# A chunked recurrence feeding two gated matmul stages: masks in one slot, the output product two tiles behind, less work ahead of step 0, and step 1's diagonals from a second set of scores

## The chip, the core and the metric

The kernel runs on one core of a Trainium2 chip. The metric is device time in microseconds (us), the median of three runs: 926.12 us before the change (925.85 to 927.89). The engines are named as in the profile: PE (TensorE), DVE (VectorE), ACT (ScalarE), POOL (GpSimd) and SP (SyncE, which issues the DMAs). Each works through its own instructions in order, and waits where an instruction's input or buffer is not ready.

## What is computed

```python
# attention-like recurrence: B=4, H=8, S=768, D=48
for t in range(S):
    cur = outer(u * k[t], v[t])                 # per head, 48x48
    y[t] = r[t] @ (state + cur)
    state = w[:, None] * state + outer(k[t], v[t])
x = y as (3072 tokens, 384)
x = (x @ w_a * x @ w_b) @ w_out                 # 384 -> 1536 -> 384
out = ((x @ w1 * x @ w2) @ w3) @ w_out2         # 384 -> 1024 -> 1024 -> 384
```

The matmul weights arrive as 64-bit floats.

## The kernel before

The recurrence is cut into 6 chunks of 128 time steps. A **unit** u = 4c + b is chunk c of batch b. For a unit the kernel computes all heads' 128x128 scores on PE (`scores`), multiplies them on DVE with a triangular mask (`a_evac`, two halves of four heads), puts the diagonal, which carries `u` in place of the decay, into them on DVE (`a_diag`, two predicated copies), and then on PE adds the state's share and the scores' share to y (`y_mm`) and forms the state's update (`s_mm`). ACT and DVE move y out of PSUM (`y_evac`), ACT decays the state (`s_decay`), DVE adds the update (`s_upd`). The diagonal's values come from `prep_d`: two POOL products and one DVE reduce. `prep_r` and `prep_k` scale r and k by powers of w, `k_nat` does it for the state's update. All of a unit's PSUM results share two buffers named `at`, so each new result waits until DVE or ACT has emptied the one two places earlier. For chunk 0 a **first block** ahead of everything does the same without a state, and takes the diagonals from a second set of scores, made with u*k (`scores_d`, `diag_0`).

**Phase 1** has six **steps** q of 512 tokens. A step is 12 tiles f of the hidden width. For each there are two *ab tiles* of nine 128x512 matmuls on PE (w_a and w_b, each in high and low float32r parts); ACT copies the first out (`g`), DVE multiplies (`ab<-g,ab`), ACT rounds to the high part (`gh`), DVE subtracts for the low part (`gl`). An *m tile*, nine more matmuls with w_out, uses gh and gl, one tile behind. During step q the units of chunk q+1 run as side work.

**The weights** are turned from 64-bit floats into pairs of float32r on the fly, in jobs of 128x512: 27 for phase 1. A job is a load; on DVE L96, L112 and L115 (bits to float32), on ACT the rounded high part (L128) and two checks (L131, L150), on DVE the low part (L148). `step()` finishes the oldest job (L148) and begins the next (L112, the L96 of the job after, L115); `cast()` issues the ACT part. An ab tile needs its three `wab` jobs; the jobs stand in the order wab0 (3), wout0 (3), wab1 (3), wab2 (3), and so on.

**The order of the work** is written out by hand. `merge` walks a step's main slots (12 x 2 ab slots and the m slots), spreads the side slots evenly over them, and in step 0 also the remaining jobs, as pairs of `step` and `cast`. A unit has eight side slots (`unit_slots`). So what an engine does between two dependent instructions is what this weaving put there.

In the first block one job begins per unit. After it come three more steps (`TAIL`), `s_mm` and `s_upd` of units 0 and 1, and three of four preparation slots of unit 4; then step 0 starts, with `s_mm` of units 2 and 3 woven in first. POOL has no other work than the preparations, and runs them as soon as their inputs are there, wherever they stand in the program.

Of the kernel before, what the change touches and what calls it, by code (L numbers as in the profile page):

```python
# [7 lines left out]
F32 = mybir.dt.float32  # L8
# [29 lines left out]

WARM, WARM_0 = 10, 6


STEPS_U = (1, 0, 0, 0)
STEPS_K = (0, 1, 1, 1)
TAIL = (1, 2)

S_NOW = 2
PRE = 3

END_0 = 4
LATE = 3  # L50
# [5 lines left out]
class Stream:  # L56
# [97 lines left out]
    def step(self):  # L154
        self.finish()
        self.begin()
# [9 lines left out]
def rwkv_moe_kernel(ctx, tc, rkT, nat, wu, wab, wout, w12, w3T, wo2, r_in, k_in, v_in, w_in, u_in, out):  # L166
# [7 lines left out]
    def flat(ap):  # L174
        return ap.rearrange("p a b -> p (a b)")

    with tc.manual_schedule():
# [41 lines left out]
        wt, ut = wt[:, 0], wt[:, 1]  # L219
        load_rk(0)  # L220
        load_nat(0)
        u_bc = const.tile([128, DM], F32, name="u_bc")

        chk = const.tile([128, N64, 2], F32, name="chk")
        small = const.tile([128, 1], F32, name="small")
# [16 lines left out]
            for k in range(KD):  # L242
                wab_ready[i] = st.add(wab[i, :, k, :], lambda k=k: dst(k))

        def add_wout(i):
# [5 lines left out]
            for j in range(3):  # L251
                s = slice(j * 512, (j + 1) * 512)
                wo_ready[i] = st.add(flat(wout[i])[:, s], lambda s=s: dst(s))

        def add_w12(i):
            w12_t[i] = [w12p.tile([128, KD, 512], F32R, name=f"w12{p}{i}") for p in "hl"]
            for k in range(KD):
                w12_ready[i] = st.add(w12[i, :, k, :], lambda k=k: [t[:, k, :] for t in w12_t[i]])

        for i in range(6):  # L260
            add_wab(i)
            if i % 2 == 0:
                add_wout(i // 2)
        st.AHEAD = 1
        for u in range(1, B):
            load_rk(u)
# [5 lines left out]
        def later_loads(u):  # L272
# [7 lines left out]
            elif u == 3:  # L280
# [8 lines left out]
        mask = const.tile([128, 128], F32, name="mask")  # L289
# [30 lines left out]
        tr = const.tile([112, NP, C], F32, name="tr")  # L320
        nc.vector.tensor_copy(out=tr[:, :, HALF:], in_=pos[:, :, 0:HALF])
        nc.vector.reciprocal(out=tr[:, :, 0:HALF], in_=pos[:, :, 1:][:, :, ::-1])
        tk = const.tile([112, NP, C], F32, name="tk")
        nc.vector.tensor_copy(out=tk, in_=tr[:, :, ::-1])
        wC = const.tile([112, NP, 1], F32, name="wC")
        nc.vector.tensor_tensor(out=wC, in0=pos[:, :, HALF:], in1=pos[:, :, HALF:], op=ALU.mult)
        s_t = [att.tile([112, NP, 112], F32, name=f"s{b}", bufs=1) for b in range(B)]

        rf_t, d_t, a_t, kn_t, at_ps, xt = {}, {}, {}, {}, {}, {}

        kf_t, pr_t, y3_t = {}, {}, {}

        def prep_r(u, eng):
            r = rk_t[u][:, 0, :]
# [116 lines left out]
        def s_mm(u):  # L451
            c, b = divmod(u, B)
            v = v_of(u)
            nat_t.pop(u, None)
            if c == NC - 1:
                return
            ps = (ps_at.tile([112, NP, D], F32, name="at") if c else
                  ps_m.tile([112, NP, D], F32, tag=("m2", "m0")[u % 2], name="s_ps"))
            at_ps["s", u] = ps
# [25 lines left out]
        def prep_slots(u):  # L485
            return [
                lambda: (prep_r(u, nc.gpsimd), prep_k(u, nc.vector)),
                lambda: prep_d(u, 0),
                lambda: prep_d(u, 1),
                lambda: prep_d(u, 2),  # L490
            ]

        def unit_slots(u):
            n = u + 1
            nxt = n < NU
            pool = nc.gpsimd

            def after(f, *a):
                if nxt:
                    f(n, *a)  # L500

            return [
                lambda: (scores(u), after(prep_r, pool)),
                lambda: (a_evac(u, 0), after(prep_k, pool)),
                lambda: (a_evac(u, 1), a_diag(u, 0), k_nat(u)),
                lambda: a_diag(u, 1),

                lambda: (y_mm(u), s_mm(u)),
                lambda: (load_rk(u + 2), load_nat(u + 2), y_evac(u), (u + 1) % B == 0 and y_shuffle(u // B), s_decay(u),
                         after(prep_d, 0)),  # L510
                lambda: (s_upd(u), after(prep_d, 1)),
                lambda: after(prep_d, 2),
            ]

# [46 lines left out]
            a_evac(u, 0)  # L561
            a_evac(u, 1)

        def steps(n):
            for _ in range(n):
                step()
                st.cast()

        prep_0(0)
        warm_up(WARM_0)  # L570
        scores_0(0)
# [8 lines left out]
        for u in range(B):  # L580
            if u + 1 < B:
                scores_0(u + 1)
                scores_d(u + 1)
            y_0(u)
            if u + 2 < B:
                prep_0(u + 2)
            if u + 1 < B:
                both_a(u + 1)
                diag_0(u + 1)
            y_0_evac(u)  # L590
            steps(STEPS_U[u])
            later_loads(u)
            if u == 2:
                tn_ps = ps_m.tile([128, NP, 112], F32, tag="m0", name="tn_ps")
                for p in range(NP):
                    mm(tn_ps[:, p, :], lhsT=tkw[:, p, :], rhs=ident[:112, :112], start=True, stop=True)
                tnat = const.tile([128, NP, 2, D], F32, name="tnat")
# [12 lines left out]


        def ab_mm(ps, w, cs, x):
# [6 lines left out]
        def ab_slots(x, wget, keep):  # L619

            t = {}

            def run_a():
                w, ca, _ = wget()
                t["a"] = ps_ab.tile([128, TB], F32, name="ab")
                ab_mm(t["a"], w, ca, x())

            def run_b():
                w, _, cb = wget()
                t["b"] = ps_ab.tile([128, TB], F32, name="ab")  # L630
                ab_mm(t["b"], w, cb, x())

            def evac_a():
                t["g"] = gp.tile([128, TB], F32, tag="g", name="g")
                nc.scalar.copy(out=t["g"], in_=t["a"])  # L635

            def evac_b():
                g = t["g"]
                gh = gp.tile([128, TB], F32R, tag="gh", name="gh")
                gl = gp.tile([128, TB], F32R, tag="gl", name="gl")  # L640
# [29 lines left out]

        def m_evac(q):
            for k in range(KD):
                t = gp.tile([128, TB], F32, tag=("g", "gh", "gl")[k], name="m_sb")
                nc.scalar.copy(out=t, in_=m_ps[q][k])
                nc.sync.dma_start(out=m_d[q][:, k, :], in_=t)

# [46 lines left out]
        for q in range(NB):  # L723
            main = []
            for f in range(NF1):
                main += ab_slots(lambda q=q: xt[q], lambda q=q, f=f: w1_get(q, f),
                                 lambda *t, q=q, f=f: gt.__setitem__((q, f), t))
                lag.append((q, f))
                if len(lag) > 1:
                    main.append(m_slot(*lag.pop(0)))  # L730
            side = step_slots(q + 1)
            if q == 0:
                side = [lambda u=u: (s_mm(u), s_upd(u)) for u in range(S_NOW, B)] + prep_slots(B)[PRE:] + side
            if q == 0:
                late = [step, st.cast] * (len(st.jobs) - st.begun + 1)
                late += [lambda: None] * (len(late) // LATE)
# [359 lines left out]
```

## Time and profile before

| | us |
|---|---|
| median of three runs | 926.12 |
| the profiled execution | 927.42 |
| its span, first to last instruction | 925.7 |
| PE busy in the span | 888.2 (96%) |
| DVE busy | 447.2 (48%) |
| ACT busy | 327.7 (35%) |
| POOL busy | 122.0 (13%) |

The shares are means over stages that differ. The first 33 us are the first block; step 0 runs until 156 us; after that PE is never without work until the last results leave, at some 919 us. A row of the timeline gives start, duration, engine, line, operation, result and inputs; in square brackets the engine's idle time ahead of it and what ended that. Consecutive like instructions are merged with a count, and instructions overlap a little at their ends, so the pace is read from start to start. PEclk is the granted TensorE clock as a share of 2.4 GHz.

### The profile page before, as it was taken

The numbers are of one execution on the slowest core, as the hardware profiler recorded it, in microseconds if no ns is written. First come the engines' busy times: TensorE is split into PE (matmuls) and PEld (weight loads), VectorE is DVE, ScalarE is ACT, GpSimd is POOL, SyncE is SP. The second block draws the span as 40 slices with busy tenths as digits, with TensorE's granted clock in tenths as the row PEclk, the third lists the DMA queues.
The fourth block names the chain that finished last, engine by engine and source line by source line (L and its number), as shares of the span: only waits on it lengthen the run. The fifth ranks groups of instructions, "written<-read, shape, count | busy, mean of one in ns | idle before, by whom it ended". The sixth has DMA issues, their size and how long they took to land.

```text
span 925.7 us, 12522 instructions
## 1 busy us (share of the span) xinstructions
PE 888.2 (96%) x4962; PEld 753.1 (81%) x4962; DVE 447.2 (48%) x745; ACT 327.7 (35%) x737; POOL 122.0 (13%) x118
## 2 busy tenths in 40 slices
PE   8488879999999999999999999999999999999997
PEld 7366668888888888888888888899988888888886
DVE  8889894444334433443333789676332323222212
ACT  4375563322222223222121687655322212122211
POOL 2512322222222312320300000000000000000000
PEclk9789989999999999999999999999999999999999
DMA  8545432211222212222103345442020201010001
GB/s 250 180 142 170 145 114 63 80 46 59 65 66 64 78 47 71 66 64 64 62 2 106 127 146 189 143 146 95 12 69 0 69 1 57 12 35 1 35 0 38
DMA packets 26066, 73.57 MB, mean 79 GB/s; under 512 B 3152, under 2 KB 7376, under 8 KB 26000
## 3 DMA queue, kind: packets, MB, share of 16 engines
q1 hardware_dynamic: 26000, 72.70, 25.2%
q8 instruction: 41, 0.67, 0.3%
q14 instruction: 25, 0.20, 0.1%
HBM read 61.28 MB, written 9.44 MB: 76 GB/s over the span
## 4 chain that ended last, share of the span: by engine, by line
PE 86%; DVE 8%; ACT 2%; DMA 2%; issue 2%; SPq 0%; ACTq 0%
PE ab L616 50%; PE m L667 5%; PE m L668 5%; PE m L669 5%; PE at L764 4%; PE o L788 3%; PE o L789 3%; PE o L787 3%; PE at L403 2%; PE at L363 2%; DVE cvt L112 2%; DVE cvt L115 2%; PE at L399 2%; DVE cvt L96 1%; DMA rk<-in_rkT_dram 1%
## 5 line engine op out<-in xcount | busy, mean ns | idle before, releaser
L641 DVE TENSOR_TENSOR ab<-g,ab 128x512 f32<-128x512 f32 x120 | 83.4, 695 | 301.2 <-PE ab L616 299.8
L616 PE MATMUL ab<-xt,w12h 128*128 128x512 f32 x576 | 177.4, 389 | 0.0
L635 ACT COPY g<-ab 128x512 f32<-128x512 f32 x120 | 70.0, 583 | 250.5 <-PE ab L616 250.5
L642 ACT CAST gh<-ab 128x512 fp32r<-128x512 f32 x120 | 70.3, 586 | 239.4 <-DVE ab L641 239.4
L616 PEld LDWEIGHTS ab<-xt,w12h 128*128 128x128 f32 x576 | 107.5, 188 | 18.8
L647 DVE TENSOR_TENSOR gl<-ab,gh 128x512 fp32r<-128x512 f32 x120 | 82.8, 690 | 65.7 <-ACT gh L642 65.5
L616 PE MATMUL ab<-xt,w12l 128*128 128x512 f32 x288 | 112.0, 389 | 0.0
L668 PE MATMUL m<-gl,woh 128*128 128x512 f32 x216 | 84.9, 393 | 1.5 <-DVE gl L647 1.5
L667 PE MATMUL m<-gh,woh 128*128 128x512 f32 x216 | 86.2, 399 | 0.0
L669 PE MATMUL m<-gh,wol 128*128 128x512 f32 x216 | 84.5, 391 | 0.0
L336 POOL TENSOR_TENSOR rk<-rk,tr 112x512 f32<-112x512 f32 x20 | 27.4, 1368 | 293.1 <-DMA rk<-in_rkT_dram 249.0
L616 PEld LDWEIGHTS ab<-xt,w12l 128*128 128x128 f32 x288 | 54.1, 188 | 11.3
L616 PE MATMUL ab<-xt,wab0h 128*128 128x512 f32 x144 | 48.5, 420 | 4.2 <-ACT xt L427 4.2
L668 PEld LDWEIGHTS m<-gl,woh 128*128 128x128 f32 x216 | 40.8, 189 | 11.1 <-DVE gl L647 2.7
L667 PEld LDWEIGHTS m<-gh,woh 128*128 128x128 f32 x216 | 40.8, 189 | 9.9 <-issue 0.4
L669 PEld LDWEIGHTS m<-gh,wol 128*128 128x128 f32 x216 | 40.7, 188 | 8.6
L115 DVE SCALAR_TENSOR_TENSOR cvt<-stg_t,cvt 128x512 int32<-128x512 int32 x61 | 47.0, 770 | 0.3
L112 DVE SCALAR_TENSOR_TENSOR cvt<-stg_t,cvt 128x512 int32<-128x512 int32 x61 | 46.9, 770 | 0.3
L616 PE MATMUL ab<-xt,wab1h 128*128 128x512 f32 x144 | 46.6, 405 | 0.0
L616 PE MATMUL ab<-xt,wab2h 128*128 128x512 f32 x144 | 45.9, 400 | 0.0
L616 PE MATMUL ab<-xt,wab3h 128*128 128x512 f32 x144 | 45.4, 396 | 0.0
L616 PE MATMUL ab<-xt,wab4h 128*128 128x512 f32 x144 | 45.3, 396 | 0.0
(271 smaller groups left out, 1579.6 us busy)
## 6 DMA issues: line engine op xcount, KB each, us to landing
natt<-in_nat_dram SPq DMA_DIRECT2D x20, 576.0 KB, 5.0
rk<-in_rkT_dram SPq DMA_DIRECT2D x24, 448.0 KB, 3.8
stg_t<-in_wab_dram SPq DMA_DIRECT2D x18, 512.0 KB, 3.7
stg_t<-in_w3T_dram SPq DMA_DIRECT2D x16, 512.0 KB, 3.6
stg_t<-in_w_dram SPq DMA_DIRECT2D x12, 512.0 KB, 3.7
stg_t<-in_wout_dram SPq DMA_DIRECT2D x9, 512.0 KB, 3.8
m_d<-m_sb SPq DMA_DIRECT2D x18, 256.0 KB, 2.2
stg_t<-m_d SPq DMA_DIRECT2D x18, 256.0 KB, 2.6
```

What stands on the lines that cost most here:

```text
L112: nc.vector.scalar_tensor_tensor(out=f, in0=w[:, :, 1], scalar=-0x40000000, in1=f, op0=ALU.bitwise_and, op1=ALU.bitwise_or)
L115: nc.vector.scalar_tensor_tensor(out=f, in0=w[:, :, 0], scalar=29, in1=f, op0=ALU.logical_shift_right, op1=ALU.bitwise_or)
L616: mm(ps, lhsT=w[i][:, k, cs], rhs=x[:, j, k, :], start=(n == 0), stop=(n == 3 * KD - 1))
L635: nc.scalar.copy(out=t["g"], in_=t["a"])
L641: nc.vector.tensor_tensor(out=t["b"], in0=g, in1=t["b"], op=ALU.mult)
L642: nc.scalar.copy(out=gh, in_=t["b"])
L647: nc.vector.tensor_tensor(out=gl, in0=t["b"], in1=gh, op=ALU.subtract)
L667: mm(m_ps[q][k], lhsT=wh[:, j, cs], rhs=gh, start=(f == 0), stop=False)
L668: mm(m_ps[q][k], lhsT=wh[:, j, cs], rhs=gl, start=False, stop=False)
L669: mm(m_ps[q][k], lhsT=wl[:, j, cs], rhs=gh, start=False, stop=(f == NF1 - 1))
L764: mm(f_ps[i], lhsT=w3_t[i][a][:, g, :], rhs=wo2_t[g // 4][b][:, g % 4, :], start=(n == 0), stop=(n == 3 * NF2 - 1))
L787: mm(o_ps[q][b], lhsT=ph[:, cs], rhs=wh, start=(f == 0), stop=False)
```

## The change

It has six parts. Line numbers in the diff's changed kernel are some 4 to 8 away from those before.

1. **First block.** `cast` goes ahead of `step`, one of each per unit; the three steps after it, its `k_nat`, `s_mm` and `s_upd` and the preparation of unit 4 are no longer there. They become side slots at the beginning of step 0, which has 42 side slots in place of 35 and 24 jobs left in place of 21.
2. **Jobs' order.** The first third of wout0 stands ahead of wab1, the other two behind it, and so on; an m tile of step 0 asks for the thirds it uses.
3. **Masks.** Both halves of the mask stand in one side slot.
4. **Diagonals of step 1** (units 4 to 7): as in the first block, from a second set of scores on PE (`scores_u`) with k scaled by u*w on ACT (`prep_u`); `prep_d`, with its two POOL products and its reduce, goes for these units. The predicated copies read PSUM.
5. **m two tiles behind** in every step, with three buffers for gh and gl.
6. Some constants move to a pool that is released after step 4.

```diff
-STEPS_U = (1, 0, 0, 0)
-STEPS_K = (0, 1, 1, 1)
-TAIL = (1, 2)
-S_NOW = 2
-PRE = 3
+STEPS = (1, 1, 1, 1)
...
         for i in range(6):
             add_wab(i)
-            if i % 2 == 0:
-                add_wout(i // 2)
+            add_wout(i // 2, ((0,), (1, 2))[i % 2])
...
+        def prep_u(u):
+            ku_t[u] = att.tile([112, NP * C], F32, name="ku", bufs=1)
+            for p in range(NP):
+                s = slice(p * C, (p + 1) * C)
+                nc.scalar.activation(out=ku_t[u][:, s], in_=kf_t[u][:, s], func=ACTF.Copy, scale=uw[:, p:p + 1])
+
+        def scores_u(u):
+            for x in range(2):
+                at_ps["d", u, x] = ps_at.tile([128, NP, C], F32, name="at")
+            scores_f([at_ps["d", u, x] for x in range(2)], flat(rf_t[u]), ku_t.pop(u))
...
+            if u < 2 * B:
+                return [
+                    lambda: (scores(u), after(prep_r, pool)),
+                    lambda: (a_evac(u, 0), a_evac(u, 1), after(prep_k, pool)),
+                    lambda: k_nat(u),
+                    lambda: scores_u(u),
+                    lambda: (diag_0(u), n < 2 * B and prep_u(n), n == 2 * B and prep_d(n, 0)),
+                    lambda: (y_mm(u), s_mm(u)),
+                    lambda: (load_rk(u + 2), load_nat(u + 2), y_evac(u), (u + 1) % B == 0 and y_shuffle(u // B),
+                             s_decay(u), n == 2 * B and prep_d(n, 1)),
+                    lambda: (s_upd(u), n == 2 * B and prep_d(n, 2)),
+                ]
...
-            steps(STEPS_U[u])
+
+            st.cast()
+            for _ in range(STEPS[u]):
+                step()
             later_loads(u)
...
-            for b in ((), (), (0, 1), (2, 3))[u]:
-                k_nat(b)
-            steps(STEPS_K[u])
-        steps(TAIL[0])
-        for u in range(S_NOW):
-            s_mm(u)
-            s_upd(u)
-        steps(TAIL[1])
-        for f in prep_slots(B)[:PRE]:
-            f()
...
-            if q == 0 and j == 0:
-                st.split(wo_ready[i])
+            if q == 0:
+                st.split(wo_ready[i, min(j, 2)])
...
-                if len(lag) > 1:
+                if len(lag) > 2:
                     main.append(m_slot(*lag.pop(0)))
             side = step_slots(q + 1)
             if q == 0:
-                side = [lambda u=u: (s_mm(u), s_upd(u)) for u in range(S_NOW, B)] + prep_slots(B)[PRE:] + side
+                side = ([lambda u=u: k_nat(u) for u in range(B)] + [lambda u=u: (s_mm(u), s_upd(u)) for u in range(B)] +
+                        prep_slots(B) + side)
```

What follows are stretches of the engines' order, before and after. On PE, ahead of and in the first ab tiles of step 0 (`s_ps`, later `at<-v,k`, is `s_mm`), before:

```order
L616 MATMUL ab<-xt,wab0h 128x512 x2
L616 MATMUL ab<-xt,wab0l 128x512
L464 MATMUL s_ps<-v_97,k_96 48x48 x8
L616 MATMUL ab<-xt,wab0h 128x512 x2
L616 MATMUL ab<-xt,wab0l 128x512
```

and now, after four ab tiles without anything between them:

```order
L620 MATMUL ab<-xt,wab0h 128x512 x2
L620 MATMUL ab<-xt,wab0l 128x512
L470 MATMUL at<-v_97,k_96 48x48 x8
L620 MATMUL ab<-xt,wab1h 128x512 x2
L620 MATMUL ab<-xt,wab1l 128x512
```

`s_mm` of unit 2 stood behind step 0's first ab tile; now the first `s_mm` stands behind the fourth, and the next tile is the first that needs wab1.

On ACT, around the first use of wab1 (`s` is `s_upd` of the first block's units, `g` and `gh` the copies of an ab pair, `CAST w..h` a job's high part), before:

```order
L483 COPY s_170<-s_ps 48x4x48 x2
L635 COPY g<-ab 128x512
L150 ACTIVATE sq,chk<-sq,small 128x512
L483 COPY s_171<-s_ps 48x4x48 x2
L642 CAST gh<-ab 128x512
L128 CAST wab1h<-cvt 128x512
```

and now:

```order
L122 CAST wab1h<-cvt 128x512
L125 ACTIVATE sq,chk<-stg_t 128x512
L144 ACTIVATE sq,chk<-sq,small 128x512
L489 COPY s_170<-at 48x4x48 x2
L489 COPY s_171<-at 48x4x48 x2
L639 COPY g<-ab 128x512
L122 CAST woh_454<-cvt 128x512
```

The high part of wout0's second third now stands behind the copies of units 1 and 2 and behind `g` of the first tile that uses wab1, the third pair.

On DVE, between the masks and the diagonals of unit 6, before (the second half of the mask, the first and the second predicated copy):

```order
L374 TENSOR_TENSOR a_sc<-at,mask 128x512
L380 COPY_PREDICATED a_sc<-ident,dg 128x512
L148 TENSOR_TENSOR wol_1078<-cvt,woh_1077 128x512
L112 SCALAR_TENSOR_TENSOR cvt<-stg_t,cvt 128x512
L96 TENSOR_SCALAR cvt<-stg_t 128x512
L115 SCALAR_TENSOR_TENSOR cvt<-stg_t,cvt 128x512
L380 COPY_PREDICATED a_sc<-ident,dg 128x512
```

and now, behind both masks and one more job (L142, L106, L90 and L109 are the old L148, L112, L96 and L115):

```order
L645 TENSOR_TENSOR ab<-g,ab 128x512
L142 TENSOR_TENSOR wab5l<-cvt,wab5h 128x512
L106 SCALAR_TENSOR_TENSOR cvt<-stg_t,cvt 128x512
L90 TENSOR_SCALAR cvt<-stg_t 128x512
L109 SCALAR_TENSOR_TENSOR cvt<-stg_t,cvt 128x512
L651 TENSOR_TENSOR gl<-ab,gh 128x512
L142 TENSOR_TENSOR wab5l<-cvt,wab5h 128x512
L106 SCALAR_TENSOR_TENSOR cvt<-stg_t,cvt 128x512
L90 TENSOR_SCALAR cvt<-stg_t 128x512
L109 SCALAR_TENSOR_TENSOR cvt<-stg_t,cvt 128x512
L396 COPY_PREDICATED a_sc<-ident,at 128x512 x2
```

One job stood between the second mask half and the last diagonal; now three jobs and the two DVE products of an ab pair do.

## Rows read from the trace of the kernel before

**Rows 1.** Stretches: busy us (instructions) of each engine, granted clock, DMA share, GB/s

```profile
33.60:130.30 96.70, 74.40 (x419) 58.57 (x420) 84.80 (x134) 61.55 (x156) 25.80 (x20) 0.84 0.47 148
130.30:156.00 25.70, 25.70 (x153) 21.16 (x152) 17.35 (x26) 11.06 (x28) 10.12 (x9) 1.00 0.23 58
156.00:500.00 344.00, 344.00 (x2080) 282.29 (x2079) 133.27 (x228) 83.97 (x184) 74.53 (x67) 1.00 0.19 56
500.00:900.00 400.00, 400.00 (x1925) 352.26 (x1924) 177.38 (x297) 154.53 (x330) 0.00 (x0) 1.00 0.22 72
```

**Rows 2.** Waits of PE in the whole span: us in total, times, longest

```profile
PE at L403 <- DVE a_sc L380: 12.1, 5, 3.2
PE s_ps L464 <- issue: 7.0, 1, 7.0
```

**Rows 3.** PE's timeline around step 0's beginning

```profile
35.32 1.39 PE L616 MATMUL ab<-xt,wab0h 128*128 128x512 f32 x2 [4.19 <-ACT xt L427]
...
46.65 0.88 PE L464 MATMUL s_ps<-v,k 128*48 128x48 f32 x16 [6.96 <-issue]
...
60.62 0.62 PE L616 MATMUL ab<-xt,wab1h 128*128 128x512 f32 x2
```

**Rows 4.** DVE's timeline at the end of the first block

```profile
32.12 1.47 DVE L115 SCALAR_TENSOR_TENSOR cvt<-stg_t,cvt 128x512 int32<-128x512 int32 x1
35.30 0.56 DVE L428 TENSOR_TENSOR xt<-at,xt 128x384 fp32r<-128x384 f32 x1 [1.71 <-ACT xt L427]
```

**Rows 5.** The end of unit 6 and the scores of unit 7, on DVE and PE

```profile
129.55 0.71 DVE L481 TENSOR_TENSOR s<-at,s 48x192 f32<-48x192 f32 x2
...
131.79 1.16 PE L363 MATMUL at<-rk 48*128 48x128 f32 x16
```

**Rows 6.** DVE's timeline: one job undisturbed, what follows it, and two waits

```profile
55.81 0.69 DVE L148 TENSOR_TENSOR wab1l<-cvt,wab1h 128x512 fp32r<-128x512 f32 x1 [1.47 <-ACT wab1h L128]
...
64.24 0.68 DVE L148 TENSOR_TENSOR wab2l<-cvt,wab2h 128x512 fp32r<-128x512 f32 x1
64.84 0.68 DVE L112 SCALAR_TENSOR_TENSOR cvt<-stg_t,cvt 128x512 int32<-128x512 int32 x1
65.44 0.41 DVE L96 TENSOR_SCALAR cvt<-stg_t 128x512 int32<-128x512 int32 x1
...
66.38 0.68 DVE L374 TENSOR_TENSOR a_sc<-at,mask 128x512 f32<-128x512 f32 x1
...
102.53 0.29 DVE L441 TENSOR_TENSOR y<-at,y 112x128 fp32r<-112x128 f32 x1 [1.88 <-ACT xt L440]
```

**Rows 7.** DVE's groups from 33.6 to 130.3 us: count, busy us, mean ns

```profile
L112 DVE SCALAR_TENSOR_TENSOR cvt<-stg_t,cvt 128x512 int32<-128x512 int32 x22 | 18.6, 844 | 0.0
L115 DVE SCALAR_TENSOR_TENSOR cvt<-stg_t,cvt 128x512 int32<-128x512 int32 x22 | 18.6, 844 | 0.0
L96 DVE TENSOR_SCALAR cvt<-stg_t 128x512 int32<-128x512 int32 x22 | 13.4, 611 | 0.0
...
L350 DVE TENSOR_REDUCE dg<-pr 128x8 f32<-128x384 f32 x4 | 2.2, 544 | 0.0
```

**Rows 8.** POOL's groups in the same stretch

```profile
L345 POOL TENSOR_TENSOR pr<-natt,u_bc 128x384 f32<-128x384 f32 x4 | 4.9, 1232 | 17.9 <-DVE dg L350 17.9
L347 POOL TENSOR_TENSOR pr<-pr,natt 128x384 f32<-128x384 f32 x4 | 4.8, 1197 | 0.3
```

**Rows 9.** The chain that ended last, one ab pair and its pace

```profile
127.75 4.12 PE ab L616 x18
```

**Rows 10.** ACT in the first block: k times u

```profile
20.83 1.26 ACT L546 ACTIVATE alt<-rk,wt 112x128 f32<-112x128 f32 x4
```

**Rows 11.** From unit 7's y to step 1: PE, and SP's DMAs of y

```profile
143.10 0.53 PE L464 MATMUL at<-natt,kn 128*48 128x48 f32 x16
...
156.02 0.62 PE L616 MATMUL ab<-xt,wab0h 128*128 128x512 f32 x2
```

**Rows 12.** SP's issue of y's six transfers at the end of step 0

```profile
144.82 5.11 SPq L448 DMA_DIRECT2D xt<-y  x6
```

More of the change, by code (lines that the diff above doesn't have):

```diff
@@ L221, in rwkv_moe_kernel @@
         load_nat(0)
-        u_bc = const.tile([128, DM], F32, name="u_bc")
+        u_bc = att.tile([128, DM], F32, name="u_bc", bufs=1)
         chk = const.tile([128, N64, 2], F32, name="chk")
@@ L243, in add_wab, with add_wout @@
                 wab_ready[i] = st.add(wab[i, :, k, :], lambda k=k: dst(k))
-        def add_wout(i):
+        def add_wout(i, part):
             def dst(s):
@@ L249, in dst @@
                 return [flat(t)[:, s] for t in wo_t[i]]
-            for j in range(3):
+            for j in part:
                 s = slice(j * 512, (j + 1) * 512)
-                wo_ready[i] = st.add(flat(wout[i])[:, s], lambda s=s: dst(s))
+                wo_ready[i, j] = st.add(flat(wout[i])[:, s], lambda s=s: dst(s))
         def add_w12(i):
@@ L288, in rwkv_moe_kernel @@
                                 base=0, pattern=[[-1, 128]], channel_multiplier=1)
-        mask = const.tile([128, 128], F32, name="mask")
+        mask = att.tile([128, 128], F32, name="mask", bufs=1)
         nc.gpsimd.memset(mask, 1.0)
@@ L319, in rwkv_moe_kernel @@
                 initial=1.0, op0=ALU.mult, op1=ALU.add)
-        tr = const.tile([112, NP, C], F32, name="tr")
+        tr = att.tile([112, NP, C], F32, name="tr", bufs=1)
         nc.vector.tensor_copy(out=tr[:, :, HALF:], in_=pos[:, :, 0:HALF])
         nc.vector.reciprocal(out=tr[:, :, 0:HALF], in_=pos[:, :, 1:][:, :, ::-1])
-        tk = const.tile([112, NP, C], F32, name="tk")
+        tk = att.tile([112, NP, C], F32, name="tk", bufs=1)
         nc.vector.tensor_copy(out=tk, in_=tr[:, :, ::-1])
@@ L326, in rwkv_moe_kernel @@
         nc.vector.tensor_tensor(out=wC, in0=pos[:, :, HALF:], in1=pos[:, :, HALF:], op=ALU.mult)
+        uw = wc
+        nc.vector.tensor_tensor(out=uw, in0=ut, in1=wc, op=ALU.mult)
         s_t = [att.tile([112, NP, 112], F32, name=f"s{b}", bufs=1) for b in range(B)]
         rf_t, d_t, a_t, kn_t, at_ps, xt = {}, {}, {}, {}, {}, {}
-        kf_t, pr_t, y3_t = {}, {}, {}
+        kf_t, ku_t, pr_t, y3_t = {}, {}, {}, {}
         def prep_r(u, eng):
@@ L456, in s_mm @@
                 return
-            ps = (ps_at.tile([112, NP, D], F32, name="at") if c else
-                  ps_m.tile([112, NP, D], F32, tag=("m2", "m0")[u % 2], name="s_ps"))
-            at_ps["s", u] = ps
+            ps = at_ps["s", u] = ps_at.tile([112, NP, D], F32, name="at")
             kn = kn_t.pop(u)
@@ L487, in prep_slots @@
                 lambda: (prep_r(u, nc.gpsimd), prep_k(u, nc.vector)),
-                lambda: prep_d(u, 0),
-                lambda: prep_d(u, 1),
-                lambda: prep_d(u, 2),
+                lambda: prep_u(u),
             ]
@@ L500, in after @@
                     f(n, *a)
+            if u < 2 * B:
[10 more added lines that the diff above has]
+                ]
             return [
                 lambda: (scores(u), after(prep_r, pool)),
-                lambda: (a_evac(u, 0), after(prep_k, pool)),
-                lambda: (a_evac(u, 1), a_diag(u, 0), k_nat(u)),
-                lambda: a_diag(u, 1),
+                lambda: (a_evac(u, 0), a_evac(u, 1), after(prep_k, pool)),
+                lambda: (a_diag(u, 0), a_diag(u, 1), k_nat(u)),
+                lambda: after(prep_d, 0),
                 lambda: (y_mm(u), s_mm(u)),
                 lambda: (load_rk(u + 2), load_nat(u + 2), y_evac(u), (u + 1) % B == 0 and y_shuffle(u // B), s_decay(u),
-                         after(prep_d, 0)),
-                lambda: (s_upd(u), after(prep_d, 1)),
+                         after(prep_d, 1)),
+                lambda: s_upd(u),
                 lambda: after(prep_d, 2),
@@ L562, in both_a @@
             a_evac(u, 1)
[L564 to L567, printed above, removed]
         prep_0(0)
@@ L596, in rwkv_moe_kernel @@
                     mm(tn_ps[:, p, :], lhsT=tkw[:, p, :], rhs=ident[:112, :112], start=True, stop=True)
-                tnat = const.tile([128, NP, 2, D], F32, name="tnat")
+                tnat = att.tile([128, NP, 2, D], F32, name="tnat", bufs=1)
                 for x, (a, e) in enumerate(XR):
                     nc.scalar.copy(out=tnat[:, :, x, :], in_=tn_ps[:, :, a:e])
-            for b in ((), (), (0, 1), (2, 3))[u]:
-                k_nat(b)
-            steps(STEPS_K[u])
-        steps(TAIL[0])
-        for u in range(S_NOW):
-            s_mm(u)
-            s_upd(u)
-        steps(TAIL[1])
-        for f in prep_slots(B)[:PRE]:
-            f()
         def ab_mm(ps, w, cs, x):
@@ L638, in evac_b @@
                 g = t["g"]
-                gh = gp.tile([128, TB], F32R, tag="gh", name="gh")
-                gl = gp.tile([128, TB], F32R, tag="gl", name="gl")
+                gh = gp.tile([128, TB], F32R, tag="gh", name="gh", bufs=3)
+                gl = gp.tile([128, TB], F32R, tag="gl", name="gl", bufs=3)
                 nc.vector.tensor_tensor(out=t["b"], in0=g, in1=t["b"], op=ALU.mult)
@@ L672, in m_evac @@
             for k in range(KD):
-                t = gp.tile([128, TB], F32, tag=("g", "gh", "gl")[k], name="m_sb")
+                t = gp.tile([128, TB], F32, tag=("g", "gh", "gl")[k], name="m_sb", bufs=(2, 3, 3)[k])
                 nc.scalar.copy(out=t, in_=m_ps[q][k])
```

## The prediction

> **What bounds the kernel now.** I read the stretches first, then PE's waits, then the timelines of DVE, ACT and PE up to 156 us. In the stretches [rows 1] PE is busy for all of 130.3 to 156 us, of 156 to 500 and of 500 to 900. Whatever the change does must therefore happen before 130 us, and a shift of PE there moves the end by the same amount. From 33.6 us, the end of the first block, to 130.3 PE works 74.4 of 96.7 us at a mean clock of 0.84 (that is, part of it at 1.2 and not at 2.4 GHz), while DVE works 84.8: in step 0 DVE is the engine to follow. PE's waits [rows 2] are of two kinds: 12.1 us before the y products, for the diagonals that DVE writes (five waits), and 7.0 us once, ahead of `s_mm` of unit 2, behind step 0's first ab tile [rows 3].
>
> The change goes at both. I ask what DVE's and ACT's queues put in their place.
>
> **The place to compare at.** Scores of unit 7 start on PE at 131.79 us [rows 5]. Ahead of them stand, in the changed order too, 18 ab tiles and 7 m tiles of step 0 and all of units 4 to 6. Behind them the same PE work is left, plus the second scores of unit 7. They need the buffer that `s_upd` of unit 6 empties, which DVE did at 130.3 us [rows 5], so PE had no wait there. If DVE reaches that instruction later than PE does, the end moves.
>
> **DVE's sum up to there.** I start at 33.6 us, the end of the third job's L115 [rows 4], since DVE's order up to it is unchanged, and count what stands in the stretch of 96.7 us before and now.
>
> - Jobs: 22 L112 and 22 L115 before [rows 7]; by the new order 24, because the remaining jobs are spread over step 0 two places earlier against the units. A job takes 2.14 us undisturbed (64.24 to 66.38 in [rows 6]): +4.3.
> - Products of the ab tiles: one pair more, eighth against ninth, at 0.60 us each by the pace of [rows 6]: +1.2.
> - Reduces: three of the four in [rows 7] end before 130.3, at 0.5 us: -1.5. The masks and predicated copies stay in number; a copy that reads PSUM has no row in step 0, and the first block's and a mask's 0.6 to 0.7 us I take for both.
> - POOL. L112 and L115 take 844 ns and L96 611 in the mean [rows 7], against 0.68 and 0.41 us undisturbed [rows 6]. That is 44 x 0.16 + 22 x 0.20 = 11.3 us lost while POOL worked 25.8 us [rows 1], 0.44 us each. The eight products of `prep_d` are 9.7 us of that [rows 8]: -4.3 us. Bounds: nothing, and 9.7.
> - The start: DVE waited 1.71 us for xt [rows 4], because ACT had the cast of the third job, and that waited for DVE, ahead of it. With cast behind, this goes: -1.7.
> - Waits. DVE idles 96.7 - 84.8 = 11.9 us, so 10.2 without that one. Two patterns carry most: a low part right behind the product of an ab pair waits for `gh` and its own cast on ACT, 1.47 us in [rows 6], and the y evacuation waits for ACT, 1.88. Counted in the order up to unit 6, the first stands three times before and five times now (+2.4). The y evacuations of units 4 to 6 meet more of an even race, PE and DVE now being in step, about 1 us each more (+3). New is the ACT stretch shown above: the cast of wout0's second third waits behind `g` of the first tile that uses wab1. PE reaches that tile early and waits for wab1, then runs it slowly after the idle time; the tile takes about twice the 2.06 us of [rows 9], 4 us, and DVE, which needs that cast next, stands for about as long (+4.4 with the copies). Smaller ones cancel with those of the three removed steps, which go (-1). Together +9. Bounds: 0, if ACT always keeps ahead, and +12, if each of the five and the three costs the 1.88 of the dearest row (+7.6) beside the 4.4.
>
> So `s_upd` of unit 6 ends at 130.3 + 4.3 + 1.2 - 1.5 - 4.3 - 1.7 + 9 = 137.3 us. PE can be there: its 74.4 us grow by three second sets of scores at 1.1 us [rows 5], into a stretch of 103.7.
>
> **PE and the rest.** Scores of unit 7 start 137.3 - 131.8 = 5.5 us later. Behind them stand the second scores of unit 7, +1.1, whose masks are ready by then (an ab pair and an m tile lie between). The wait ahead of the scores and the one ahead of unit 6's y (below) leave PE at the low clock for some us, which before had passed by 130 [rows 1]; I take +1.0, between 0 and 2.5. Sum: +7.6.
>
> What becomes of the two removed waits: the 7.0 us at `s_mm` go, and PE does four ab tiles from about 34 us. Then it needs wab1, four jobs further on DVE. These end at about 52 us (40 for the fourth job's start, slowed by POOL as before, then four low parts and three starts, 7, three products, 1.8, and waits, 3) and not at 60.6 [rows 3]; four tiles are 8.2 us [rows 9], some 11 with the low clock, so PE waits some 6 us there instead. The waits for diagonals shrink for units 4 and 5, but of unit 6 they don't: between its masks and its diagonals DVE now has three jobs and two products (6.4 + 1.2, with waits 9), PE three tiles and a set of scores, 7.3. That is about 4 us. In addition each unit now has one more return trip from PE to DVE.
>
> At nothing I cost: ACT's k times u*w, 1.26 us for a unit [rows 10], in ACT's 35 us of room [rows 1] (without it, up to 5 us more of what is in the term for waits); the jobs' order and the m tile two behind, which are the same PE work, in later steps hidden by a PE that never waits; the pools. Of `k_nat` and the preparations of unit 4 POOL runs the same ones at the same time, their inputs deciding, so DVE's slow stretch at 30 to 40 us stays but for 2 us of `prep_d`. Unit 7's y must reach step 1: 12.4 us lie between [rows 11], an m tile fewer now, 10.3; SP's issues end 6.3 us after unit 7 [rows 11, 12], so a landing within 4 us is free, else up to 2 us: I take 0.
>
> **A rule against the POOL term.** The rows give 0.44 us of DVE's loss for one of POOL's work [rows 1, 7]. The Trainium skill (SBUF — State Buffer, "Who interferes with whom") says that a DVE instruction with two SBUF inputs and a GpSimd instruction that reads SBUF block each other fully. L112 and L115, which read two SBUF tiles, agree as far as they are the slowed ones. By the rule the removed POOL work would give back up to its whole length, 9.7 and not 4.3.
>
> **Sum.** The profiled execution took 927.4 us, so 935.0; against the median of 926.1 it is 933.7. I forecast 933.7 us.
>
> **Rivals.**
> - *POOL's whole time comes back* (5.4 us more), or half of the waits do not come: `s_upd` of unit 6 at about 132, scores of unit 7 on time, the second scores and a little clock remain, +2: 928. For it speaks that four instructions in a row can be slowed by POOL; against it the mean of 0.44.
> - *Faster: ACT keeps ahead of DVE*, so DVE waits no longer than before. Then unit 6 ends at 128.3, PE is held by nothing at the scores of unit 7, and gains 3.5 less 1.1: 923.7. It decides where the casts find ACT free: from about +5 us of waits the gain is gone. For it: the 7 us and most of the 12 us that PE lost have other reasons than DVE's total. Against it: the new order itself, casts behind `g`.
> - *Dearer*: the upper bound of the waits (+3), the clock (+1.5) and y's transfers (+2) together: 940.
> - That the change doesn't remove the waits it goes at: for the y of unit 6 that is in the forecast; for all units, 936.
>
> **Chances.** Forecast (929.5 to 937, the fourth rival with it) 0.64; 928 with its neighbours 0.14, of which 0.11 lie within 0.2% (1.85 us, about what can be told from no change); faster 0.14, of which 0.01 is within; dearer 0.08. So faster 0.13, same 0.12, slower 0.75. The range goes from 924 to 939; the forecast's own is 929.5 to 937.
>
> **What would show it.** Right: the first ab tile near 34 us; a PE wait of 5 to 7 us ahead of the first wab1 tile, that at 50 to 54; a DVE low part idle for 3 to 5 us on ACT soon after; unit 7's scores at 135 to 139, ahead of them a wait for DVE; PE without waits from there on. Wrong: unit 7's scores before 131 us, or DVE's idle time up to them at 12 us or less; or a wait of PE in a later step, which nothing here foresees.

## The result, and the profile after

The changed kernel takes 936.6 us (median of 4 runs, 935.84 to 940.46) against 926.5 for the kernel before on the same chip: a ratio of 1.012, 95% interval 1.0103 to 1.0137. It is slower by about 10 us; the forecast was slower by 7.6. The profiled execution took 935.8 us, 8.4 more than the one of before.

The stretches of the changed kernel, from the end of DVE's third job to unit 7's scores, then as in [rows 1] (columns as there):

```profile
29.30:137.60 108.30, 79.53 (x507) 62.00 (x506) 89.26 (x141) 71.33 (x183) 26.25 (x19) 0.88 0.49 155
130.30:156.00 25.70, 20.68 (x132) 16.82 (x131) 13.42 (x20) 8.19 (x20) 5.38 (x6) 0.87 0.15 46
156.00:500.00 344.00, 344.00 (x2065) 282.31 (x2064) 132.47 (x227) 84.17 (x184) 79.27 (x72) 1.00 0.19 58
500.00:900.00 400.00, 400.00 (x1935) 351.71 (x1934) 177.46 (x298) 155.32 (x332) 0.00 (x0) 1.00 0.22 72
```

From 156 us on PE is full, as before: all that is lost is lost in step 0. PE's idle time is now 28.8 us of 108.3 (22.3 of 96.7 before), and DVE's is 19.0 (11.9 before). POOL works 26.25 us in the stretch, where it worked 25.80, although the eight products of [rows 8] are gone.

PE's waits from 28 to 160 us, against [rows 2]:

```profile
PE at L359 <- DVE s L487: 7.5, 3, 5.0
PE at L407 <- DVE a_sc L396: 6.1, 1, 6.1
PE ab L620 <- ACT wab1h L122: 5.1, 2, 2.8
PE at L359 <- DVE a_sc L370: 3.4, 1, 3.4
PE ab L620 <- ACT g L639: 3.1, 1, 3.1
PE at L359 <- ACT sq L125: 2.5, 1, 2.5
```

The two old waits are gone. In place of the 7.0 us at `s_mm` PE waits for the first wab1 tile, first for `g`, to empty a buffer, and then twice for the job. In place of the five waits for diagonals there is one of 6.1, and waits for `s_upd` (L487) and for the masks (L370), all of which DVE writes; the last row, ahead of unit 4's scores, the profile puts down to ACT. On PE's timeline:

```profile
28.89 0.50 PE L620 MATMUL ab<-xt,wab0h 128*128 128x512 f32 x1 [0.57 <-ACT xt L435]
...
45.64 1.22 PE L620 MATMUL ab<-xt,wab1h 128*128 128x512 f32 x2 [2.78 <-ACT wab1h L122]
...
108.42 1.13 PE L359 MATMUL at<-rk 48*128 48x128 f32 x14 [1.83 <-DVE s L487]
...
123.39 2.05 PE L407 MATMUL at<-rk,s 112*112 112x128 f32 x8 [6.14 <-DVE a_sc L396]
...
137.70 2.05 PE L359 MATMUL at<-rk 48*128 48x128 f32 x14 [5.02 <-DVE s L487]
```

The last row is unit 7's scores, at 131.79 in [rows 5]: 5.9 us later, behind 5.02 us of waiting for `s_upd` of unit 6. What DVE did ahead of that:

```profile
128.04 0.29 DVE L449 TENSOR_TENSOR y<-at,y 112x128 fp32r<-112x128 f32 x1 [1.68 <-ACT xt L448]
...
130.25 0.69 DVE L645 TENSOR_TENSOR ab<-g,ab 128x512 f32<-128x512 f32 x1 [1.46 <-PE ab L620]
132.11 2.08 DVE L142 TENSOR_TENSOR wol<-cvt,woh 128x512 fp32r<-128x512 f32 x1 [1.17 <-ACT woh L122]
134.11 1.48 DVE L106 SCALAR_TENSOR_TENSOR cvt<-stg_t,cvt 128x512 int32<-128x512 int32 x1
...
136.83 0.72 DVE L487 TENSOR_TENSOR s<-at,s 48x192 f32<-48x192 f32 x2
```

This is the loop in small. PE was 6.14 us late with unit 6's y, because DVE was late with its diagonals; so PE's next ab tile is late, DVE waits 1.46 us for it and 1.17 for the cast that ACT has behind it, two DVE instructions beside POOL's next preparation (131.68 to 135.04) take two and three times as long as in [rows 6], and PE waits 5.02 us for the `s_upd` at the end of that row. Each engine in turn pays for the others' delay.

Step 1's first ab tile starts at 162.86 us (156.02 in [rows 11]). One more m tile is still owed there, 2.06 us, so PE is 8.9 us behind, and it stays so: PE's last matmul starts at 927.47 against 918.66, 8.8 later.

### The profile page after: what moved, and what is told of

Its sections match the earlier page's. It is cut to its first block, busy times and chain, and to the rows that moved or that the text cites. A ratio compares the mean times of both kernels' runs of the same rounds, so it can differ in the third digit from the quotient of the medians.

```text
span 934.1 us, 12649 instructions
## 1 busy us (share of the span) xinstructions
PE 893.9 (96%) x5026; PEld 757.2 (81%) x5026; DVE 440.4 (47%) x742; ACT 334.0 (36%) x753; POOL 113.7 (12%) x110
## 4 chain that ended last, share of the span: by engine, by line
PE 87%; DVE 7%; ACT 2%; issue 2%; DMA 1%; SPq 0%; POOL 0%; ACTq 0%; DVEq 0%; POOLq 0%
PE ab L620 50%; PE m L671 5%; PE m L672 5%; PE m L673 5%; PE at L769 4%; PE o L793 3%; PE o L794 3%; PE o L792 3%; PE at L359 3%; PE at L411 2%; DVE cvt L106 2%; PE at L407 2%; DVE cvt L109 2%; DVE cvt L90 1%; PE at L794 1%
## 5 line engine op out<-in xcount | busy, mean ns | idle before, releaser
L620 PEld LDWEIGHTS ab<-xt,w12l 128*128 128x128 f32 x288 | 54.1, 188 | 11.3
L620 PE MATMUL ab<-xt,wab0h 128*128 128x512 f32 x144 | 45.6, 397 | 1.0 <-ACT xt L435 0.6
L106 DVE SCALAR_TENSOR_TENSOR cvt<-stg_t,cvt 128x512 int32<-128x512 int32 x61 | 46.4, 760 | 0.3
L620 PE MATMUL ab<-xt,wab5h 128*128 128x512 f32 x144 | 45.1, 395 | 0.0
```

The costliest lines, as they stand in the source:

```text
L106: nc.vector.scalar_tensor_tensor(out=f, in0=w[:, :, 1], scalar=-0x40000000, in1=f, op0=ALU.bitwise_and, op1=ALU.bitwise_or)
L620: mm(ps, lhsT=w[i][:, k, cs], rhs=x[:, j, k, :], start=(n == 0), stop=(n == 3 * KD - 1))
```

## The experiments

Two theories to begin with. A: the first block's early work (part 1 of the change), put into step 0, makes DVE the late engine there. B: the second scores with their return trips (part 4), the longer lag of m, or casts behind `g` make it. Each ratio is to runs of the kernel before on the same chip, whose medians were 925.8 to 926.2 us; what an edit gives back is the difference of two ratios, 1.012 for the changed kernel.

**e1: diagonals of units 4 to 7 by `prep_d` again.**

```diff
-            if u < 2 * B:
+            if False:
                 return [
...
-                lambda: prep_u(u),
+                lambda: prep_d(u, 0),
+                lambda: prep_d(u, 1),
+                lambda: prep_d(u, 2),
```

> The changed kernel with the diagonals of units 4 to 7 from prep_d again, as before the change (no second scores, eight side slots a unit as in the later chunks; everything else as changed). Theory A (DVE's queue: the weaving of jobs, casts and unit slots sets when unit 7's scores can start, the second scores cost only what stands behind that point): 4.4 us of PE work go, of which one set, 1.1 us, stood on the path, DVE gets four reduces (2.2 us) and POOL eight products back; 934 to 937 us, PE's wait ahead of unit 7's scores stays at 3 us or more. Theory B (the second scores, with their PE time and their extra return trip per unit, are the cause): 926 to 929 us.

931.05 us, ratio 1.0055 (1.0038 to 1.0072), between the two ranges. PE's wait ahead of unit 7's scores, which theory A had stay, is gone (`s_upd` of unit 6 starts at 134.13, the scores at 136.02); the one for unit 6's diagonals is still there, 4.7 us in place of 6.1.

**e3: m one tile behind** (`len(lag) > 1`):

> The changed kernel with m one tile behind again. Theories A and B: 935 to 939 us; m tiles between the units' instructions come one earlier, nothing else. A third theory C, that the later m tiles leave PE without work it could do while it waits: 928 to 932 us.

930.77 us, ratio 1.0047 (1.003 to 1.0064): in the range of theory C, outside that of A and B. e5 below comes back to C.

**e4: in step 0's slots the due cast ahead of `g` and `gh`:**

```diff
-                for g in f[1:2]:
+                if first and at2 < (i + 1) * len(late) // len(main) and late[at2] == st.cast:
+                    late[at2]()
+                    at2 += 1
+                for g in f[1:2]:
```

> The changed kernel with, in step 0's main slots, a cast that is due put on ACT ahead of the slot's g or gh instead of behind it (nothing else moves on DVE or PE). Theory A: the five DVE waits of 1.2 us and the one of 2.2 us at wout0 go, up to 8 us of DVE time ahead of unit 7's scores, so 928 to 933 us. Theory B: 935 to 938 us, DVE's idle time being a consequence of PE's.

931.07 us, ratio 1.0049 (1.0033 to 1.0066). Three unlike edits give back 0.65, 0.73 and 0.71%, some 6 to 7 us each. That could be three causes of equal size, or one cause that each relieves.

**e2: the first block as before**, all else as changed (all of unit 4's preparation ahead of step 0):

```diff
-            st.cast()
-            for _ in range(STEPS[u]):
+            for _ in range((1, 0, 0, 0)[u]):
                 step()
+                st.cast()
...
+            for b in ((), (), (0, 1), (2, 3))[u]:
+                k_nat(b)
+            for _ in range((0, 1, 1, 1)[u]):
+                step()
+                st.cast()
+        step()
+        st.cast()
+        for u in range(2):
+            s_mm(u)
+            s_upd(u)
+        for _ in range(2):
+            step()
+            st.cast()
+        for f in prep_slots(B):
+            f()
...
-                side = ([lambda u=u: k_nat(u) for u in range(B)] + [lambda u=u: (s_mm(u), s_upd(u)) for u in range(B)] +
-                        prep_slots(B) + side)
+                side = [lambda u=u: (s_mm(u), s_upd(u)) for u in range(2, B)] + side
```

> The changed kernel with part 1 undone: seven steps ahead of step 0, k_nat, s_mm and s_upd of units 0 and 1 and the preparation of unit 4 ahead of it, so 36 side slots and 21 jobs in step 0; second scores, masks together, m two behind, the new job order stay. Theory A: the units stand wider apart and fewer jobs stand between their instructions; 927 to 931 us, DVE's idle time up to unit 7's scores back to 10 to 13 us. Theory B: 933 to 937 us, since the second scores are still there.

924.41 us, ratio 0.9983 (0.997 to 0.9997): 1.37%, 12.7 us back, more than the whole loss, and below theory A's range. (The medians alone give 11.7 us back.)

**b1: the kernel before with part 1 alone** (`cast` and `step` once per unit; its `k_nat`, `s_mm`, `s_upd` and preparation as side slots, which makes 44 side slots, nine more than before and not thirteen; its `s_mm` uses the `at` buffers, as in the changed kernel):

> The kernel before with part 1 alone: one cast and one step per unit in the first block, and nothing between it and step 0 (k_nat, s_mm, s_upd and the preparations become 13 more side slots; 24 jobs in step 0); diagonals, masks, m one behind, job order as before. If part 1 alone makes the loss (theory A): 932 to 938 us. If the loss needs part 1 together with the second scores or the later m, so that each alone is hidden by slack (theory D, a threshold): 925 to 930 us.

938.03 us, ratio 1.0113 (1.0088 to 1.0138). PE's waits there are again for what DVE writes: 12.1 us in seven places for the diagonals, 5.8 in two for `s_upd`.

**b2: the kernel before with the second scores alone**:

> The kernel before with the second scores alone for units 4 to 7 (masks still in two slots, second scores and copies in the slots behind, preparation of unit 4 all ahead of step 0). Theory A: 922 to 927 us, POOL's eight products and three reduces go and the second scores' 4.4 us lie in time in which PE waits anyway. Theory B: 929 us or more.

927.27 us, ratio 1.0011 (0.9999 to 1.0022), between the ranges of A and B.

Part 1 alone makes the whole loss within the intervals (b1), and with all the rest of the change but without part 1 there is none (e2). Theory B falls: e1, e3 and e4 relieve, they don't cause. The three were not put together in one run.

Part 1 has two halves: three jobs more to do in step 0, and eight more side slots at its beginning (42; e2 has 34), which push every unit back against tiles and jobs.

**e7: three more jobs ahead of step 0**, side slots as changed. The edit also puts `step` ahead of `cast` in the first block again, as e2 does:

```diff
-            st.cast()
-            for _ in range(STEPS[u]):
+            for _ in range((1, 0, 0, 0)[u]):
                 step()
+                st.cast()
...
+            for _ in range((0, 1, 1, 1)[u]):
+                step()
+                st.cast()
+        for _ in range(3):
+            step()
+            st.cast()
```

> The changed kernel with three more jobs begun ahead of step 0 (seven as before, 21 left in the step and not 24); k_nat, s_mm, s_upd and the preparation of unit 4 stay side slots of step 0. Theory A (part 1 costs by the jobs: three more at 2.1 us on DVE, with their casts on ACT): most of the loss goes, 926 to 930 us. Theory B (part 1 costs by the eight side slots more, which push every unit later against the tiles): 933 to 937, since the jobs then only move.

934.23 us, ratio 1.0082 (1.0069 to 1.0096), in theory B's range.

**e8: `k_nat`, `s_mm` and `s_upd` of units 0 and 1 and the preparation ahead of step 0**, jobs as changed:

```diff
+            for b in ((), (), (0, 1), (2, 3))[u]:
+                k_nat(b)
+        for u in range(2):
+            s_mm(u)
+            s_upd(u)
+        for f in prep_slots(B):
+            f()
...
-                side = ([lambda u=u: k_nat(u) for u in range(B)] + [lambda u=u: (s_mm(u), s_upd(u)) for u in range(B)] +
-                        prep_slots(B) + side)
+                side = [lambda u=u: (s_mm(u), s_upd(u)) for u in range(2, B)] + side
```

> The changed kernel with the side slots of before (k_nat, s_mm and s_upd of units 0 and 1, the preparation of unit 4 ahead of step 0) and the jobs as changed: four begun ahead of it, 24 left in the step. Theory A (the jobs): 932 to 936 us. Theory B (the side slots): 925 to 929. If each half gives about 5 to 6 us, as three other single edits did, it is again one relief among several, and neither half alone is the cause.

929.36 us, ratio 1.0045 (1.0031 to 1.0058), just above theory B's range. Of e2's 1.37% the jobs, with the order of `cast` and `step`, give back 0.38 alone and 0.62 on top of the side slots; the side slots give back 0.75 alone and 0.99 on top of the jobs. So the side slots carry the larger part, and neither half alone reaches the time of before.

From step 0's first ab tile to unit 7's scores, the stretches of the changed kernel, e7, e8 and e2, in this order (columns as in [rows 1]):

```profile
28.89:137.70 108.81, 79.94 (x508) 62.22 (x508) 89.77 (x141) 71.39 (x184) 26.66 (x19) 0.88 0.49 155
```

```profile
34.01:136.43 102.42, 83.02 (x508) 65.22 (x508) 84.75 (x140) 69.63 (x181) 19.86 (x14) 0.87 0.46 139
```

```profile
31.81:123.97 92.16, 75.11 (x469) 57.85 (x465) 77.80 (x128) 64.26 (x167) 16.56 (x12) 0.93 0.57 173
```

```profile
35.32:122.50 87.18, 75.20 (x469) 58.99 (x467) 74.73 (x129) 64.96 (x168) 12.76 (x10) 0.91 0.53 162
```

The third busy number (DVE) tells it. Where the side slots are as changed, DVE has 140 or 141 instructions to do before unit 7 may start; where they are as before, 128 or 129. In the first two one more ab pair and two more jobs stand ahead of unit 7. None of the work that moved into the side slots but one `prep_k` product, which all four have, runs on DVE (`k_nat` is on POOL, `s_mm` on PE, `s_upd` of these units and `prep_u` on ACT), so what DVE has more is work that now comes before the units. The fifth (POOL) falls from 26.7 to 12.8 us when the products of the first block's `k_nat` and unit 4's preparation stand ahead of the stretch. Of the three bit-moving groups of DVE, in the changed kernel and in e2:

```profile
L106 DVE SCALAR_TENSOR_TENSOR cvt<-stg_t,cvt 128x512 int32<-128x512 int32 x24 | 21.0, 874 | 0.0
L109 DVE SCALAR_TENSOR_TENSOR cvt<-stg_t,cvt 128x512 int32<-128x512 int32 x25 | 19.5, 780 | 0.0
L90 DVE TENSOR_SCALAR cvt<-stg_t 128x512 int32<-128x512 int32 x23 | 12.6, 548 | 0.0
```

```profile
L106 DVE SCALAR_TENSOR_TENSOR cvt<-stg_t,cvt 128x512 int32<-128x512 int32 x22 | 17.2, 781 | 0.0
L109 DVE SCALAR_TENSOR_TENSOR cvt<-stg_t,cvt 128x512 int32<-128x512 int32 x22 | 15.0, 682 | 0.0
L90 DVE TENSOR_SCALAR cvt<-stg_t 128x512 int32<-128x512 int32 x22 | 10.8, 492 | 0.0
```

At 0.68 and 0.41 us [rows 6] these take 42.8 and 38.9 us; the rest, 10.3 and 4.1, I put down to POOL. The jobs' low parts lose in the same way (25 take 19.9 us, and 22 in e2 16.4, at 0.68 each), which makes 13.2 and 5.4. DVE's busy time is 15.0 us less in e2, 7.8 of it by that and 7.2 by less work (jobs and the ab pair); its idle time is 6.6 less (19.0 and 12.5). Step 0 starts 6.4 later there, and so unit 7's scores come 15.2 earlier. PE then has 3.3 us more to do until step 1 (28.5 against 25.2). That leaves 11.9: step 1's first ab tile starts at 151.01 us and not at 162.86, and the profiled executions differ by 11.4 (924.4 and 935.8).

The last four look for what remains.

**e5: e2 with m one tile behind:**

> The run with part 1 undone, and m one tile behind as well. Theory C (the later m is bad in itself): 2 us or more faster than with m two behind (924.4). Theories A and D (the later m costs only when DVE holds PE up at every unit): 922 to 926 us, no difference beyond 1.5 us.

925.87 us, ratio 0.9999 (0.9985 to 1.0012): the later m costs nothing in itself, so theory C falls.

**e9: e2 with the casts of e4:**

> The kernel with the first block as before (924.4 us) and in addition the due cast ahead of g and gh in step 0's slots. If the waits of DVE for casts behind g still cost there, 921 to 923. If with the first block as before DVE has slack, nothing: 924 to 925. If the cast now holds g back (g later, PE waits for its ab buffer): 926 to 928.

924.09 us, ratio 0.998 (0.9971 to 0.9989).

**e10: e2 with the diagonals of e1:**

> The kernel with the first block as before and in addition the diagonals of units 4 to 7 by prep_d again: only the jobs' order, the masks together and the m tile two behind are left of the change. If the second scores gain by themselves once DVE isn't late (1.1 us of PE a unit against 3 us of waits for diagonals): 926 to 929. If they cost what they bring, as on the kernel before: 924 to 925. If the second scores were the dearer way (5.5 us as in the changed kernel): 919 to 921.

925.52 us, ratio 1.0002 (0.9993 to 1.0011).

What gave 0.65 to 0.73% in the changed kernel gives -0.16, 0.03 and -0.19% here, and each interval overlaps that of e2. The three were relief for one shortage; where DVE is less late they have little to relieve.

**e6: a mixture**, the changed kernel with casts ahead of steps and of `g`, three more steps, `k_nat` and unit 4's preparation ahead of step 0, all four `s_mm` in it:

> What the runs so far would have combined: the changed kernel with cast ahead of step in the first block (as changed), the three more steps, k_nat and the preparation of unit 4 ahead of step 0 (as before), all four s_mm as side slots (as changed), and a due cast ahead of g or gh in step 0. Theory A: all of the DVE waits named so far get shorter, 915 to 923 us. If PE's waits for s_upd and the diagonals have another cause: 924 us or more.

930.37 us, ratio 1.0033 (1.0016 to 1.005): a miss. The first `s_mm` there waits on PE as it did before the change [rows 3], but longer, and the two waits of the changed kernel return, for unit 6's diagonals (5.8 us) and, ahead of unit 7's scores, for `s_upd`:

```profile
49.24 0.88 PE L470 MATMUL at<-v,k 128*48 128x48 f32 x16 [11.76 <-issue]
...
131.68 2.04 PE L359 MATMUL at<-rk 48*128 48x128 f32 x14 [3.57 <-DVE s L487]
```

The best of all are e2 and e9, which their intervals don't tell apart: both about 0.2% faster than the kernel before.

## Why the prediction was right

The mechanism held: DVE reaches `s_upd` of unit 6 later than PE reaches unit 7's scores, and the end moves by that. Unit 7's scores were forecast at 137.3 us and came at 137.7. But two terms of the sum were off, each by 4.3 us, and cancelled, in part by luck. Point by point:

- **The start, step "I start at 33.6 us, the end of the third job's L115 [rows 4], since DVE's order up to it is unchanged": wrong by 4.3 us.** DVE's third job ends at 29.3, not 33.6, and PE's first ab tile is at 28.89, not 34. On DVE, where [rows 4] has L115 at 32.12 for 1.47 us:

```profile
28.64 0.67 DVE L109 SCALAR_TENSOR_TENSOR cvt<-stg_t,cvt 128x512 int32<-128x512 int32 x1
29.25 0.54 DVE L436 TENSOR_TENSOR xt<-at,xt 128x384 fp32r<-128x384 f32 x1
```

  The order is the same, but in this execution the job ran ahead of POOL's `k_nat` (28.31 to 34.19 us) and not beside it, and the wait for xt went, as forecast (1.7). The job's four instructions take 2.42 us here and took 5.11 before: 2.7 of the 4.3. The other 1.6 are the trace of before: its third job starts at 28.70 us, and that of every other trace, with either first block, between 26.8 and 27.7. In e4, whose first block is the changed one, `k_nat` starts at 26.80 and the job ends at 32.2: it is a race. PE's early first tile isn't: it comes at 28.7 to 29.5 us in all six traces in which `cast` stands ahead of `step` and no `s_mm` ahead of step 0 (e4 among them), and at 32.3 to 35.3 in all seven with `step` ahead of `cast`.
- **The POOL term, -4.3: not there.** The eight products did go, but POOL worked 26.25 us in the stretch and 25.80 before [rows 1]: `k_nat` of the first block (5.9 us), one `kn` more (1.0) and unit 8's two diagonal products (2.3) now fall into it. POOL's rows for that, from 29.3 to 137.6 us:

```profile
L352 POOL TENSOR_TENSOR k<-k,tnat 128x384 f32<-128x384 f32 x4 | 5.9, 1498 | 10.2 <-ACT tnat L613 10.2
L352 POOL TENSOR_TENSOR kn<-natt,tnat 128x384 f32<-128x384 f32 x4 | 4.8, 1212 | 0.0
L343 POOL TENSOR_TENSOR pr<-pr,natt 128x384 f32<-128x384 f32 x1 | 1.3, 1324 | 0.1
L341 POOL TENSOR_TENSOR pr<-natt,u_bc 128x384 f32<-128x384 f32 x1 | 1.0, 986 | 0.0
```

  DVE's loss in the three groups was 11.6 us [rows 7] (11.3 in the prediction, by rounding) and is 10.3; with the low parts, which are slowed too and which the prediction left out, it was 13.1 and is 13.2. Most of what should have come back is the slowing that left the start: `k_nat` cost the third job 2.7 us ahead of 33.6 before, and costs the fourth, whose four instructions take 4.97 us, 2.5 behind 29.3 now. To that extent the two errors are one and had to cancel; that the rest, 1.6 us of the trace of before against unit 8's products, cancelled too is luck. The step that failed is "POOL runs the same ones at the same time, their inputs deciding, so DVE's slow stretch at 30 to 40 us stays but for 2 us of `prep_d`": POOL's part was so, but DVE was at another place beside it. The rival that all of POOL's time comes back falls with it. The Trainium skill (SBUF — State Buffer, "Who interferes with whom") has a DVE instruction with two SBUF inputs and a GpSimd one that reads SBUF block each other fully. The mean over the stretch, 0.39 us lost in the three groups for each one of POOL's, is no test of that, since it counts POOL's time beside an idle DVE too. Where the groups and low parts ran beside POOL, for 22.6 us, they lost 13.2. Part of the rest may be POOL's loss: `k_nat`'s four products took 5.88 us here and 4.94 before.
- **Jobs +4.3, ab pair +1.2, reduces -1.5: right.** 24, 25 and 23 of the three groups, 9 products and no reduce stand there. With the loss to POOL unchanged, DVE's busy time had to grow by 4.0; it grew by 4.5.
- **Waits +9: right as a sum, 19.0 us of idle time against a forecast of 19.2, with parts too large and too small.** DVE's waits from 28 to 140 us, the first five:

```profile
DVE wol L142 <- ACT woh L122: 5.2, 4, 2.2
DVE y L449 <- ACT xt L448: 4.9, 3, 2.0
DVE wab1l L142 <- ACT wab1h L122: 2.3, 2, 1.2
DVE ab L645 <- PE ab L620: 1.5, 1, 1.5
DVE wab5l L142 <- ACT wab5h L122: 1.4, 2, 1.2
```

  The y evacuations cost 3.0 more than the one of before, as forecast, and low parts right behind a product wait 1.17 us in five rows, the first at 39.76 us and the last at 132.11. The wait behind `g` of the first wab1 tile was 2.2 and not 4.4; a wait of 1.5 for PE at a product, which the forecast had put into no row, and more of the low parts' smaller waits fill that up.
- **PE's waits.** Some 6 us at the first wab1 tile: 5.1 and, ahead of it, 3.1 for `g`, from 39 to 50 us; the tile's last third starts at 49.65 (50 to 54 forecast). About 4 us at unit 6's diagonals: 6.1. The waits for `s_upd` of earlier units, for masks and ahead of unit 4's scores were not forecast.
- **Behind unit 7's scores.** Second scores +1.1 as forecast; the clock cost 1.9, by difference, and not 1.0. From 5.9 us at the scores (5.5 forecast) to 8.9 at step 1 (7.6 forecast) these two make 3.0. y's transfers cost nothing, and PE waits nowhere behind the scores, as forecast.
- **The faster rival, ACT ahead of DVE**, was tried in part by e4: with casts ahead of `g` DVE idles 15.1 us up to unit 7's scores (103.3 less 88.2 busy), 4 less than in the changed kernel, and the kernel is still 0.49% slower than before.
- **The fourth rival**, that the waits stay (for all units, 936), names the time nearest to the measured one, but not what happened: the waits for the diagonals of units 4 and 5 are gone, and those for `s_upd` and the masks came in their place. The dearer one (940) didn't come, y's transfers costing nothing.

What the prediction didn't see is why the sum came out so: not the products, scores and copies that the change is about, but part 1: 42 side slots where 35 stood and, with a smaller share (e7, e8), 24 jobs where 21 stood. It counted the two jobs and the pair that this puts ahead of unit 7, as +5.5 us, but took the change as one piece and asked of no part what the rest would be without it. e2 and b1 show that this part decides the sign.

What stays open: how part 1's cost divides between its halves to the last. e7 and e8 give back 0.38 and 0.75%, the 0.24 that come only with both are of the size of the intervals, and no run moves the jobs without the order of `cast` and `step`. Nor does a run tell the eight slots as such from the work that stands in them on PE, ACT and POOL: empty slots were not tried.

## What to carry to other kernels

Where two engines run neck and neck, price a reordering by what the later engine has to do, its waits included, before the next dependent piece may start; a wait that is removed comes back at the next such place unless that sum falls. When early work is woven into a later stage, the slots that it takes there move the dependent work behind it (here by two jobs and an ab pair), and slowing by a third engine moves along with the work. And before believing that several single edits each win the same few per mille, undo them on a variant without the shortage: here three reliefs of 0.7% each were worth nothing there.

## What the chip showed beside that

Like work of PE cost by what stood ahead of it. Unit 6's scores at 108.42, behind 1.83 us of idle time, took 1.13 us at a granted clock of 1.00; unit 7's at 137.70, behind 5.02, took 2.05 at 0.50, the lower of the two levels (1.2 GHz).

A predicated copy from PSUM, which no row of step 0 showed before, costs what one from SBUF did, before and now:

```profile
L380 DVE COPY_PREDICATED a_sc<-ident,dg 128x512 f32<-128x512 int32 x6 | 4.3, 724 | 0.0
L396 DVE COPY_PREDICATED a_sc<-ident,at 128x512 f32<-128x512 int32 x6 | 4.1, 732 | 0.0
```

Of POOL these rows tell nothing, because none of these copies, and no mask, ran beside a POOL instruction. The products of the ab tiles, which read PSUM too, did, and were not slowed (their 18 rows of the stretch take 0.68 to 0.69 us in the mean): one on DVE, with the POOL product that ran all the while,

```profile
105.83 2.34 POOL L332 TENSOR_TENSOR rk<-rk,tr 112x512 f32<-112x512 f32 x1 [18.11 <-DMA rk<-in_rkT_dram]
106.96 0.68 DVE L651 TENSOR_TENSOR gl<-ab,gh 128x512 fp32r<-128x512 f32 x1
```

and 0.69 us at 130.25, where the low part behind it, with both inputs in SBUF, took 2.08 beside POOL, three times its 0.68.
